# Moving elementwise work between VectorE, GpSimd and ScalarE in a fused attention, convolution and MLP kernel

## The chip, the cores and the metric

One core of a Trainium2 chip runs the whole program. The metric is the device time of one execution in microseconds; the median of several executions is compared.

## The reference

Three blocks follow one another. The batch is 4, the sequence 544 (32 global and 512 local tokens), the width 512.

1. Attention: 8 heads of 64; global queries see all keys, local queries see the global keys and a window of 32 to each side.
2. A gated MLP with a convolution: `h = relu(x @ w_in)` to 1024 columns, a convolution of three taps over the sequence, `sigmoid` of it as a gate, `(h * gate) @ w_out` back to 512.
3. A block with a Fourier transform over sequence and features, of which the real part is added: `u = x + real(fft(fft(x)))`, then a layer norm, `relu(un @ w_ch1) @ w_ch2` through 2048 columns (the dense MLP), and `u + ch`.

The weights and most other inputs reach the kernel as float64 in HBM and are turned into float32 on the chip.

## The kernel before, in words

**Precision.** Products are made in float32 halves: a value is split into a high part in float32r (a rounded copy by ScalarE) and the rest (value minus high part, a subtraction of two tensors), and `mm3` (L144) makes three matmuls of the two. So each weight tile and each activation needs a copy and a two-tensor subtraction.

**Weights.** `fetch` (L177) loads 128 x 512 float64 values as pairs of int32; `from_f64` (L161) makes float32 of them in place. Its steps: ScalarE takes the absolute value of the head word (L163); a clamp to the range of float32 (L164); the tail word is shifted right by 29 bits (L168 on VectorE, or L166 on ScalarE as an arithmetic scaling); VectorE joins both (L170); VectorE puts the sign in (L175), or ScalarE makes a sign tensor (L172) and GpSimd multiplies by it (L173). `put` (L201) then makes the high part by ScalarE (L203) and the rest by GpSimd (L204). There are 16 such tiles for `w_in` and `w_out` (`make_w`, L427; for `w_out` a sum and a difference of halves come between, L433 and L434) and 32 for `w_ch1` and `w_ch2` (`make_c`, L698, one tile, and `make_cs`, L713, two or three tiles at once with L719 in place of L204). The intermediate value lies in `mag`, of which there are two buffers; late in the kernel three buffers cut from `misc` take their place.

**Stages.** The first loop (L543) runs over 32 halves of head pairs plus two. Each step makes scores (`s_mm`), a masked maximum on VectorE (L279), the exponential on ScalarE (L291), a scaling on GpSimd (L302), transposes on TensorE, copies out of PSUM (L321) and the product with the values. In steps 0 to 7 the tiles of `w_in` and `w_out` are converted beside it. From step 10 on each step also does two units of the gated MLP (64 units in all): `m_g1` (first product, L453 evacuates on ScalarE), `m_conv` (three taps: L464 or L466 for the middle one, L467, L468), `m_tanh` (L474), `m_gate` (L485 to L487) and `m_g2` (second product). From unit 52 the middle tap is on ScalarE (L464), before on VectorE (L466).

A second loop (L820) ends the gated MLP; the first batch's transform (`fft`, L616) and the first layer norm (`ln(0)`, L724) run beside it, and the first eight tiles of `w_ch1` are fetched and converted. The third loop (L859) is the dense MLP: 128 units in 8 pieces of half a batch (`c_g1` L767, evacuated by L779 and L780; `c_g2` L783, accumulated over 16 units and finished by L800, L801). In its first five units the transforms of the other three batches and the next twelve conversions are done, in the next units the last twelve; `ln(c + 1)` runs in the midst of piece `c`.

**The transform.** `fft` folds a batch into its even and odd parts (L623, L626 on GpSimd, L627 one row on VectorE), splits these (L624, L625, L628, L629), multiplies with cosine and sine tables over features and then tokens, evacuates (L642 to L650, L663 to L676) and adds and subtracts the results into `u` (L677 on VectorE, L678 on GpSimd). `ln` sums features (L733, L734), multiplies by ones on TensorE, subtracts the mean (L742), splits (L743, L744 on GpSimd), squares (L747) and sums again (L749, L750), and makes the reciprocal root (L760, L761). `ln(1)` and later use the space of the last transform's input as scratch.

**What sets the order.** In the first loop the order of TensorE and of the DMA queue of SyncE is that of the program text; on the other engines, and on all engines after that loop, a planner places instructions by the priorities of the table at L21 and by its own estimates of time. Each engine then executes its list in order. All large loads are issued on SyncE's queue, the transform's tables on GpSimd's (L805).

Of the kernel before, what the change touches and what calls it, by code (L numbers as in the profile page):

```python
# [28 lines left out]
NF = 274  # L29
# [95 lines left out]
def fused_kernel(ctx: ExitStack, tc: tile.TileContext, d, out):  # L125
# [35 lines left out]
    def from_f64(raw, mag, clamp=None, tail_act=False, sign_act=False):  # L161
        head, tail = raw[:, :, 1], raw[:, :, 0]
        act.activation(mag, f32(head), AF.Abs, scale=65536.0)  # L163
        (clamp or dve).tensor_scalar(mag, mag, 2.0, TOP, op0=ALU.max, op1=ALU.min)  # L164
        if tail_act:
            act.activation(tail, tail.bitcast(U32), AF.Copy, scale=0.999 * 2.0**-29, bias=-0.499)  # L166
        else:
            dve.tensor_scalar(tail, tail, 29, None, op0=ALU.logical_shift_right)  # L168
        val = bits(mag)
        dve.scalar_tensor_tensor(val, val, 3, tail, op0=ALU.logical_shift_left, op1=ALU.bitwise_or)  # L170
        if sign_act:
            act.activation(f32(head), f32(head), AF.Sign)  # L172
            gp.tensor_mul(mag, mag, f32(head))  # L173
        else:
            dve.scalar_tensor_tensor(val, head, -(2**31), val, op0=ALU.bitwise_and, op1=ALU.bitwise_or)  # L175
# [25 lines left out]
    def put(pool, tag, val):  # L201
        t = pool.tile([128, 2, 512], F32R, tag=tag, name="w_" + tag)
        act.copy(t[:, 0], val)  # L203
        gp.tensor_sub(t[:, 1], val, f32(t[:, 0]))  # L204
        return t
# [220 lines left out]
    @prio("w")  # L426
    def make_w(i):  # L427
        val = unpack(mp, w_raw.pop(i), gp if i >= 8 else dve)
        if i < 8:
            w_in[i] = put(wp, f"w{i}", val)  # L430
            return
        eo = mp.tile([128, 512], F32, tag="mag", name="mag", bufs=2)
        dve.tensor_add(eo[:, 0:256], val[:, 0:256], val[:, 256:512])  # L433
        gp.tensor_sub(eo[:, 256:512], val[:, 0:256], val[:, 256:512])  # L434
        w_out[i - 8] = put(wp, f"w{i}", eo)
# [20 lines left out]
    def m_conv(u):  # L456
# [6 lines left out]
        if u >= 52:  # L463
            act.mul(y, hb[:, cc:cc + HS], convw2[:, m, 1:2])  # L464
        else:
            dve.tensor_scalar(y, hb[:, cc:cc + HS], convw2[:, m, 1:2], None, op0=ALU.mult)  # L466
# [149 lines left out]
    def fft(b):  # L616
# [6 lines left out]
        gp.tensor_add(fe, eo[:, 0:2, 0:NF], eo[:, 0:2, rev])  # L623
        act.copy(fh[:, 0:2], fe)  # L624
        gp.tensor_sub(fl[:, 0:2], fe, f32(fh[:, 0:2]))  # L625
        gp.tensor_sub(fd, eo[:, 2:4, 0:NF], eo[:, 2:4, rev])  # L626
        dve.tensor_add(fd[0:1, 0], eo[0:1, 2, 0:NF], eo[0:1, 2, rev])  # L627
        act.copy(fh[:, 2:4], fd)  # L628
        gp.tensor_sub(fl[:, 2:4], fd, f32(fh[:, 2:4]))  # L629
# [26 lines left out]
        for c in range(2):  # L656
# [21 lines left out]
            gp.tensor_sub(ut[:, 2 + c, 0:S], e[:, 0:S], q[:, 0:S])  # L678
# [18 lines left out]
    @prio("cv")  # L697
    def make_c(i):  # L698
        t = put(*c_slot(i), unpack(mp, w_raw.pop(i), dve, i > 15, i % 3 == 0))
        if i < 16:  # L700
            ch1[i] = t
        else:
            ch2[i - 16] = t
# [8 lines left out]
    @prio("cv")  # L712
    def make_cs(i, k):  # L713
        raw = w_raw.pop(i)
        vals = [unpack(mp, raw[:, j], dve, True, (i + j) % 3 == 0) for j in range(k)]
        t = fp.tile([128, k, 2, 512], F32R, tag=f"v{i}", name="ws")
        for j in range(k):
            act.copy(t[:, j, 0], vals[j])
            gp.tensor_sub(t[:, j, 1], vals[j], f32(t[:, j, 0]))  # L719
            ch2[i + j - 16] = t[:, j]  # L720
# [3 lines left out]
    def ln(c):  # L724
# [8 lines left out]
        gp.tensor_add(s4, ut[:, 0:2], ut[:, 2:4])  # L733
        gp.tensor_add(s4[:, 0], s4[:, 0], s4[:, 1])  # L734
# [9 lines left out]
        gp.tensor_sub(cl, cf, f32(ch))  # L744
# [4 lines left out]
        gp.tensor_add(s4, cf[:, 0:2], cf[:, 2:4])  # L749
        gp.tensor_add(s4[:, 0], s4[:, 0], s4[:, 1])  # L750
# [175 lines left out]
```

## Time and profile before

| what | value |
|---|---|
| median of 3 runs | 882.42 us (882.37 to 883.85) |
| the profiled execution | 884.08 us, of which 881.9 us span |
| TensorE busy (matmul) | 803.3 us, mean granted clock 0.940 |
| VectorE busy | 505.4 us, 1222 instructions |
| ScalarE busy | 347.4 us, 884 instructions |
| GpSimd busy | 308.6 us, 318 instructions |

The span goes from the first to the last instruction of the profiled execution; what lies around it belongs to the execution's time too. In the rows PE is TensorE's matmuls, PEld its weight loads, DVE VectorE, ACT ScalarE, POOL GpSimd, SP SyncE. L164 is line 164 of the kernel before. The granted clock is TensorE's, as a share of 2.4 GHz. A group's idle time is that of its engine just before these instructions, with what ended most of it.

### The profile page before, as it was taken

The page shows a single profiled execution, that of the slowest core. Times are in us where ns is not written, and L with a number is a line of the kernel's source. Part 1 is how long each engine was busy: PE and PEld are TensorE (multiplying, and loading weights), DVE is VectorE, ACT ScalarE, POOL GpSimd, SP SyncE. Part 2 cuts the span into 40 slices and gives each one's busy share as a digit, 9 for nine tenths or more (in the row PEclk, how much of TensorE's full clock was granted, in tenths as well). Part 3 has the DMA queues.
Part 4 walks back from the last instruction along what each step waited for, and adds up shares of the span by engine and source line. Part 5 has one row for each costly group of instructions (what it writes and reads, how often), then busy time and mean ns, then how long its engine had stood idle before and what let it go on. Part 6 is the DMA issues. An engine that isn't in the chain of part 4 may idle for free. (4 is left out here: it accounts for less than half of the span.)

```text
span 881.9 us, 16202 instructions
## 1 busy us (share of the span) xinstructions
PE 803.3 (91%) x6436; PEld 752.0 (85%) x6436; DVE 505.4 (57%) x1222; ACT 347.4 (39%) x884; POOL 308.6 (35%) x318
## 2 busy tenths in 40 slices
PE   5767999999999999987779489999999999999997
PEld 3445788999899899877678388999999999999997
DVE  5786977686778767899788973221222222222212
ACT  4555555555555534555446552112121212121110
POOL 4878622132222222564676656022130404030100
PEclk8776999999999999989779699999999999999999
DMA  9460111101010012253304300000000000000000
GB/s 315 139 205 15 72 34 53 60 29 58 30 59 29 2 40 66 72 165 99 143 0 159 129 1 26 1 26 1 14 14 1 26 1 27 1 26 1 27 1 25
DMA packets 25387, 48.33 MB, mean 55 GB/s; under 512 B 1960, under 2 KB 18728, under 8 KB 25312
## 3 DMA queue, kind: packets, MB, share of 16 engines
q1 hardware_dynamic: 24480, 44.66, 15.0%
q0 software_dynamic: 832, 2.65, 1.2%
q8 instruction: 50, 0.82, 0.4%
q14 instruction: 25, 0.20, 0.1%
HBM read 43.23 MB, written 4.46 MB: 54 GB/s over the span
## 5 line engine op out<-in xcount | busy, mean ns | idle before, releaser
L302 POOL TENSOR_SCALAR pb<-pb,sm 128x224 f32<-128x224 f32 x128 | 72.9, 585 | 153.0 <-DVE sm L297 107.0
L142 PE MATMUL ps_a<-hdt,w_v 128*128 128x272 f32 x864 | 122.1, 290 | 0.0
L142 PE MATMUL ps_a<-g,w_w 128*128 128x272 f32 x768 | 114.1, 295 | 6.2 <-ACT g L486 4.4
L142 PE MATMUL ps_g<-xh,w_w 128*128 128x274 f32 x512 | 115.0, 303 | 0.0
L142 PEld LDWEIGHTS ps_a<-hdt,w_v 128*128 128x128 f32 x864 | 114.6, 191 | 0.0
L142 PE MATMUL ps_pv<-chl,w_w 128*128 128x272 f32 x768 | 109.7, 291 | 4.0 <-DVE hdt L780 3.8
L142 PE MATMUL ps_g<-chl,w_w 128*128 128x272 f32 x768 | 109.1, 290 | 2.4 <-DVE hdt L780 2.4
L142 PEld LDWEIGHTS ps_a<-g,w_w 128*128 128x128 f32 x768 | 103.2, 192 | 8.0 <-ACT g L486 5.2
L142 PEld LDWEIGHTS ps_pv<-chl,w_w 128*128 128x128 f32 x768 | 102.1, 191 | 5.3 <-issue 4.1
L142 PEld LDWEIGHTS ps_g<-chl,w_w 128*128 128x128 f32 x768 | 101.8, 190 | 3.1 <-DVE hdt L780 3.1
L780 DVE SCALAR_TENSOR_TENSOR hdt<-ps_pv,hdt 128x272 fp32r<-128x272 f32 x64 | 28.2, 440 | 122.0 <-ACT hdt L779 121.9
L142 PE MATMUL ps_a<-hdt,ws 128*128 128x272 f32 x672 | 92.5, 287 | 1.7 <-POOL ws L719 1.7
L801 POOL TENSOR_TENSOR misc<-misc,u 128x272 f32<-128x272 f32 x28 | 19.3, 720 | 212.6 <-DVE misc L800 212.6
L142 PEld LDWEIGHTS ps_g<-xh,w_w 128*128 128x128 f32 x512 | 86.7, 193 | 7.7 <-issue 4.4
L780 DVE SCALAR_TENSOR_TENSOR hdt<-ps_g,hdt 128x272 fp32r<-128x272 f32 x64 | 28.0, 437 | 109.2 <-ACT hdt L779 109.2
L142 PEld LDWEIGHTS ps_a<-hdt,ws 128*128 128x128 f32 x672 | 87.2, 188 | 1.9 <-POOL ws L719 1.9
L779 ACT ACTIVATE hdt<-ps_g 128x272 fp32r<-128x272 f32 x64 | 25.4, 397 | 128.1 <-PE ps_g L142 125.5
L779 ACT ACTIVATE hdt<-ps_pv 128x272 fp32r<-128x272 f32 x64 | 25.3, 395 | 128.0 <-PE ps_pv L142 127.1
L142 PE MATMUL ps_g<-xl,w_w 128*128 128x274 f32 x256 | 75.2, 294 | 0.0
L291 ACT ACTIVATE pb<-pb,sm 128x224 f32<-128x224 f32 x128 | 60.2, 472 | 15.6 <-DVE sm L279 15.6
L474 ACT ACTIVATE y<-y 128x272 f32<-128x272 f32 x64 | 27.5, 430 | 76.2 <-DVE y L468 76.2
L142 PE MATMUL ps_s<-qk 64*128 64x224 f32 (+1 forms) x144 | 40.1, 431 | 16.4 <-DVE smg L373 9.3
(211 smaller groups left out, 1489.4 us busy)
## 6 DMA issues: line engine op xcount, KB each, us to landing
qk<-in_qk_dram SPq DMA_DIRECT2D x16, 592.0 KB, 5.6
raw_w<-in_ch_dram SPq DMA_DIRECT2D x16, 512.0 KB, 3.8
v<-in_v_dram SPq DMA_DIRECT2D x8, 640.0 KB, 4.8
raw_v<-in_ch_dram SPq DMA_DIRECT2D x9, 512.0 KB, 5.8
out_dram<-misc SPq DMA_DIRECT2D x32, 136.0 KB, 1.8
raw_w<-in_w_in_dram SPq DMA_DIRECT2D x8, 512.0 KB, 5.1
raw_w<-in_w_out_dram SPq DMA_DIRECT2D x8, 512.0 KB, 4.0
raws<-in_ch_dram SPq DMA_DIRECT2D x7, 512.0 KB, 5.1
```

Source lines behind the costliest of these rows:

```text
L142: return pe.matmul(o, a, b, start=start, stop=stop)
L291: act.activation(p, p, AF.Exp, bias=sm[:, k:k + 1], scale=-1.0, accum_out=sm[:, 4 + k:5 + k])
L302: gp.tensor_scalar(p, p, sm[:, k:k + 1], 1.0, op0=ALU.mult, op1=ALU.mult)
L474: act.activation(g_t[u], g_t[u], AF.Tanh, scale=0.5)
L779: act.activation(hd[:, 0], o, AF.Relu)
L780: dve.scalar_tensor_tensor(hd[:, 1], o, 0.0, f32(hd[:, 0]), op0=ALU.max, op1=ALU.subtract)
L801: (dve if c == 7 else gp).tensor_add(o, o, u_t[b][:, e, HS * half:HS * half + HS])
```

## The change

Two-tensor additions and subtractions go from GpSimd to VectorE in the weight conversions, the transforms, and the layer norm of piece 0 (`eng` in `ln`; later pieces stay on GpSimd). The clamps of all 48 weight tiles are done by GpSimd (16 of them in `make_w`, of which 8 were there before). The shift of the tail word goes to ScalarE for all 32 tiles of `w_ch1` and `w_ch2` (before: the 16 of `w_ch2`) and for the even ones of the 16 of `w_in` and `w_out` (before: none). The variant with a sign tensor, used by every third tile of the 32, is gone: VectorE puts all signs in. All middle taps of the convolution are on ScalarE. The clamp's two operations are written in the other order.

```diff
-    def from_f64(raw, mag, clamp=None, tail_act=False, sign_act=False):
+    def from_f64(raw, mag, clamp=None, tail_act=False):
...
-        (clamp or dve).tensor_scalar(mag, mag, 2.0, TOP, op0=ALU.max, op1=ALU.min)
+        (clamp or dve).tensor_scalar(mag, mag, TOP, 2.0, op0=ALU.min, op1=ALU.max)
...
-        if sign_act:
-            act.activation(f32(head), f32(head), AF.Sign)
-            gp.tensor_mul(mag, mag, f32(head))
-        else:
-            dve.scalar_tensor_tensor(val, head, -(2**31), val, op0=ALU.bitwise_and, op1=ALU.bitwise_or)
+        dve.scalar_tensor_tensor(val, head, -(2**31), val, op0=ALU.bitwise_and, op1=ALU.bitwise_or)
...
     def put(pool, tag, val):
-        gp.tensor_sub(t[:, 1], val, f32(t[:, 0]))
+        dve.tensor_sub(t[:, 1], val, f32(t[:, 0]))
...
     def make_w(i):
-        val = unpack(mp, w_raw.pop(i), gp if i >= 8 else dve)
+        val = unpack(mp, w_raw.pop(i), gp, i % 2 == 0)
...
-        gp.tensor_sub(eo[:, 256:512], val[:, 0:256], val[:, 256:512])
+        dve.tensor_sub(eo[:, 256:512], val[:, 0:256], val[:, 256:512])
...
     def m_conv(u):
-        if u >= 52:
-            act.mul(y, hb[:, cc:cc + HS], convw2[:, m, 1:2])
-        else:
-            dve.tensor_scalar(y, hb[:, cc:cc + HS], convw2[:, m, 1:2], None, op0=ALU.mult)
+        act.mul(y, hb[:, cc:cc + HS], convw2[:, m, 1:2])
...
     def fft(b):
-        gp.tensor_add(fe, eo[:, 0:2, 0:NF], eo[:, 0:2, rev])
+        dve.tensor_add(fe, eo[:, 0:2, 0:NF], eo[:, 0:2, rev])
         act.copy(fh[:, 0:2], fe)
-        gp.tensor_sub(fl[:, 0:2], fe, f32(fh[:, 0:2]))
-        gp.tensor_sub(fd, eo[:, 2:4, 0:NF], eo[:, 2:4, rev])
+        dve.tensor_sub(fl[:, 0:2], fe, f32(fh[:, 0:2]))
+        dve.tensor_sub(fd, eo[:, 2:4, 0:NF], eo[:, 2:4, rev])
...
-        gp.tensor_sub(fl[:, 2:4], fd, f32(fh[:, 2:4]))
+        dve.tensor_sub(fl[:, 2:4], fd, f32(fh[:, 2:4]))
...
-            gp.tensor_sub(ut[:, 2 + c, 0:S], e[:, 0:S], q[:, 0:S])
+            dve.tensor_sub(ut[:, 2 + c, 0:S], e[:, 0:S], q[:, 0:S])
...
     def make_c(i):
-        t = put(*c_slot(i), unpack(mp, w_raw.pop(i), dve, i > 15, i % 3 == 0))
+        t = put(*c_slot(i), unpack(mp, w_raw.pop(i), gp, True))
...
     def make_cs(i, k):
-        vals = [unpack(mp, raw[:, j], dve, True, (i + j) % 3 == 0) for j in range(k)]
+        vals = [unpack(mp, raw[:, j], gp, True) for j in range(k)]
...
-            gp.tensor_sub(t[:, j, 1], vals[j], f32(t[:, j, 0]))
+            dve.tensor_sub(t[:, j, 1], vals[j], f32(t[:, j, 0]))
...
     def ln(c):
+        eng = gp if c else dve
-        gp.tensor_add(s4, ut[:, 0:2], ut[:, 2:4])
-        gp.tensor_add(s4[:, 0], s4[:, 0], s4[:, 1])
+        eng.tensor_add(s4, ut[:, 0:2], ut[:, 2:4])
+        eng.tensor_add(s4[:, 0], s4[:, 0], s4[:, 1])
...
-        gp.tensor_sub(cl, cf, f32(ch))
+        eng.tensor_sub(cl, cf, f32(ch))
...
-        gp.tensor_add(s4, cf[:, 0:2], cf[:, 2:4])
-        gp.tensor_add(s4[:, 0], s4[:, 0], s4[:, 1])
+        eng.tensor_add(s4, cf[:, 0:2], cf[:, 2:4])
+        eng.tensor_add(s4[:, 0], s4[:, 0], s4[:, 1])
```

## Rows read from the trace of the kernel before

**Rows 1.** Stretches: busy us (count) of PE, PEld, DVE, ACT, POOL, then granted clock

```profile
22.00:110.00 88.00, 66.42 (x508) 50.98 (x504) 69.51 (x199) 48.23 (x133) 67.16 (x71) 0.77 0.33 108
132.00:330.00 198.00, 198.00 (x1855) 181.60 (x1855) 147.59 (x465) 106.72 (x324) 46.67 (x85) 1.00 0.12 39
330.00:540.00 210.00, 170.60 (x1150) 156.69 (x1150) 177.22 (x278) 108.92 (x221) 122.92 (x80) 0.88 0.27 89
375.00:419.00 44.00, 35.71 (x228) 32.55 (x227) 43.92 (x69) 25.71 (x53) 24.16 (x14) 0.88 0.43 132
485.00:507.00 22.00, 8.98 (x47) 7.55 (x47) 21.55 (x23) 12.16 (x22) 15.24 (x10) 0.61 0.35 130
540.00:870.00 330.00, 330.00 (x2640) 330.00 (x2640) 77.69 (x159) 60.48 (x137) 55.15 (x55) 1.00 0.04 13
```

**Rows 2.** What TensorE waited for, 330 to 540: total us, times, longest

```profile
PE ps_t L142 <- DVE hdt L736: 9.7, 2, 8.9
```

**Rows 3.** Order of time, 483.5 to 487: start us, us, instruction

```profile
483.94 1.85 POOL L678 TENSOR_TENSOR u<-u 128x544 f32<-128x544 f32 x1
484.50 1.57 DVE L164 TENSOR_SCALAR misc<-misc 128x512 f32<-128x512 f32 x1
```

**Rows 4.** Durations of L164 and L677, whole span: min/median/max ns

```profile
L164 DVE TENSOR_SCALAR misc<-misc x24: 406/414/2732, 404.0 to 528.6; 128x512 f32<-128x512 f32 x24
L164 POOL TENSOR_SCALAR mag<-mag x8: 1913/1915/2462, 15.1 to 101.1; 128x512 f32<-128x512 f32 x8
L677 DVE TENSOR_TENSOR u<-u x8: 706/1205/1903, 361.2 to 490.4; 128x544 f32<-128x544 f32 x8
```

**Rows 5.** Order of time at two GpSimd clamps, 27.5 to 30.6, 100.9 to 103

```profile
27.89 2.46 POOL L164 TENSOR_SCALAR mag<-mag 128x512 f32<-128x512 f32 x1 [0.80 <-ACT mag L163]
27.90 0.68 DVE L175 SCALAR_TENSOR_TENSOR mag<-raw_w,mag 128x512 int32<-128x512 int32 x1
...
101.05 1.92 POOL L164 TENSOR_SCALAR mag<-mag 128x512 f32<-128x512 f32 x1 [0.80 <-ACT mag L163]
101.09 0.87 DVE L467 SCALAR_TENSOR_TENSOR y<-h,convw,y 128x272 f32<-128x272 f32 x1
```

**Rows 6.** Groups of VectorE, 330 to 540: busy us, mean ns, idle before

```profile
L164 DVE TENSOR_SCALAR misc<-misc 128x512 f32<-128x512 f32 x24 | 18.5, 772 | 5.8 <-ACT misc L163 5.8
L164 DVE TENSOR_SCALAR mag<-mag 128x512 f32<-128x512 f32 x8 | 6.5, 810 | 0.0
L168 DVE TENSOR_SCALAR raw_w<-raw_w 128x512 int32<-128x512 int32 x16 | 10.7, 673 | 1.8 <-DMA raw_w<-in_ch_dram 1.8
L170 DVE SCALAR_TENSOR_TENSOR mag<-mag,raw_w 128x512 int32<-128x512 int32 x8 | 5.4, 680 | 0.0
L677 DVE TENSOR_TENSOR u<-u 128x544 f32<-128x544 f32 x8 | 10.2, 1277 | 0.0
```

**Rows 7.** Tile y, two stretches: busy us (count) of DVE, ACT, then granted clock

```profile
132.00:330.00 198.00, 95.39 (x201) 33.89 (x80) 1.00 0.12 39
330.00:540.00 210.00, 44.12 (x66) 19.43 (x44) 0.88 0.27 89
```

**Rows 8.** Busy time of L170, then of L175, 330 to 540

```profile
330.00:540.00 210.00, 29.73 (x32) 0.88 0.27 89
330.00:540.00 210.00, 21.80 (x21) 0.88 0.27 89
```

**Rows 9.** Groups of GpSimd, 330 to 540

```profile
L744 POOL TENSOR_TENSOR chl<-u,chl 128x1088 fp32r<-128x1088 f32 x3 | 10.4, 3452 | 7.0 <-ACT chl L743 7.0
```

**Rows 10.** Groups of GpSimd, 0 to 132

```profile
L204 POOL TENSOR_TENSOR w_w<-mag,w_w 128x512 fp32r<-128x512 f32 x16 | 22.2, 1395 | 5.6 <-ACT w_w L203 2.8 <-issue 2.7
L164 POOL TENSOR_SCALAR mag<-mag 128x512 f32<-128x512 f32 x8 | 16.4, 2054 | 5.4 <-ACT mag L163 5.3
L434 POOL TENSOR_TENSOR mag<-mag 128x256 f32<-128x256 f32 x8 | 6.6, 826 | 6.3 <-DVE sm L296 3.8 <-DVE sm L297 1.6 <-DVE mag L175 0.7
```

**Rows 11.** What VectorE waited for, 0 to 132: total us, times, longest

```profile
DVE mag L170 <- POOL mag L164: 3.0, 1, 3.0
```

## The prediction, made before the changed kernel was seen

> **What bounds the kernel now.** I read the table of stretches first [rows 1]. From 132 to 330 us and from 540 to 870 us TensorE is busy without a break at granted clock 1.00, which is its upper level, 2.4 GHz: nothing that is done on VectorE, ScalarE or GpSimd can shorten these 528 us. What can move is the start (22 to 110: TensorE 66.4 of 88, clock 0.77) and the middle (330 to 540: 170.6 of 210, clock 0.88). In the middle VectorE is busy 177.2 of 210 us, and 43.9 of 44 and 21.6 of 22 in the two densest pieces; in the second of these TensorE works 9 of 22 us at 0.61, mostly its lower level of 1.2 GHz, after standing idle. Then I read who TensorE waits for there: the longest wait, 8.9 us, is for VectorE's L736 [rows 2]. So the middle is paced by VectorE, and the reader should ask what VectorE's time consists of.
>
> A part of it is waiting inside its instructions. In order of time [rows 3]: GpSimd's subtraction L678 runs from 483.94 to 485.79; VectorE's clamp L164 starts at 484.50 and is done at 486.07, 0.28 us after GpSimd. It took 1.57 us where its median is 0.41 [rows 4]. So beside a two-tensor instruction of GpSimd VectorE's instruction stood until that ended. The change takes most of these away. Whether it puts something as bad in their place is seen where GpSimd clamps already [rows 5]: its clamp ran from 27.89 to 30.35, and VectorE's two-tensor L175, started 0.01 us after it, took 0.68 us, as long as such an instruction takes undisturbed (0.680, the row of L170 on mag in [rows 6]). At 101.05 a second clamp ran 1.92 us; L467, started 0.04 us after, took 0.87 us, longer than the 0.475 that its kind takes on average from 132 to 330 [rows 7], but not the 1.9 of the clamp. The clamp itself can lose: 2.46 us against a median of 1.92 [rows 4].
>
> Against this speaks a rule of the Trainium skill, page "SBUF — State Buffer", section "SBUF: two separate sides": GpSimd's instruction and a VectorE instruction with two SBUF inputs take one port pair as an exclusive lock for their whole length. By it the longer clamps would block as the additions do. The two clamps above disagree; it is rival A.
>
> **The change part by part, on VectorE in the middle stretch.**
> 1. Clamps to GpSimd: 32 leave, 18.5 + 6.5 = 25.0 us [rows 6]. Shifts to ScalarE: 16 leave, 10.7 us [rows 6]. Together 35.7 us.
> 2. Waiting that ends inside what stays. L170: 29.73 us for 32, at 0.680 each 21.8, so 8.0 waiting; L175: 21.80 for 21, so 7.5 [rows 8]. L677: 8 × (1.277 − 0.706) = 4.6 [rows 4, 6]. The convolution and gate (tile y): 0.668 us each here (44.12 over 66) against 0.475 (95.39 over 201) in 132 to 330, where GpSimd did almost no two-tensor work [rows 7]; 66 × 0.19 is 12.8, of which I take 10, since the short middle tap is a fifth of the instructions there and rare here. Sum 30. What stays on GpSimd are the layer norms of pieces 1 and up, whose L744 is 10.4 us for three [rows 9], and the final additions, about a tenth of its 122.9 us [rows 1]. So 27 us of waiting go.
> 3. Added: 32 subtractions of 512 columns at 0.68 = 21.8; the sign by VectorE for the 11 tiles that used ScalarE and GpSimd, 11 × 0.68 = 7.5; the FFTs' six additions of 544 to 548 columns for four batches, 24 × 0.71 (the undisturbed L677 [rows 4]) = 17.0; the layer norm of piece 0, 0.71 + 0.44 + 1.4 + 0.71 + 0.44, scaled by columns, about 3.6. Together 49.9.
> Net: 49.9 − 35.7 − 27 = −12.8 us of VectorE's time. The bounds: none of the waiting goes, +14; all of it goes and the moved additions cost only 0.6, about −20. I take the middle, as the two clamps and the L678 row lie on that side. VectorE is busy in 84% of the stretch, so the stretch gives back 0.84 × 12.8 = **10.8 us**. TensorE allows it: it idles 39.4 us there, and some more is lost to the clock.
>
> GpSimd loses about 100 of its 122.9 us and gets 32 clamps at about 2.05 (mean of eight [rows 10]), 65.6 us: it stays below half busy. ScalarE gets 16 shifts and is rid of 11 signs on the same shape, at 108.9 of 210 [rows 1]: nothing, as long as VectorE is the fuller engine.
>
> The new waits: a tile's second VectorE step now waits for a GpSimd clamp and its last for a ScalarE copy. Behind a waiting VectorE stand the convolution, the FFT evacuations and L780, so TensorE. Eight clamps on GpSimd cost VectorE one wait of 3.0 us [rows 11], 0.38 each: 32 would cost 12. Today VectorE waits for ScalarE before its own clamp; that goes to GpSimd. From −6 to +12, I take zero: seven of eight cost nothing. In the three-buffer part a tile's chain grows by 1.9 − 0.4 for the clamp and shrinks by 1.4 − 0.7 for the subtraction; that 0.8 us I cost at nothing, since loads and conversions stand several tiles ahead, and with that cover gone 12 us at most (16 tiles).
>
> **The start (0 to 132).** GpSimd loses 16 subtractions (22.2) and 8 halves (6.6) and gets 8 clamps (16.4): −12.4 us [rows 10]. VectorE gets 16 × 0.68 and 8 halves at some 0.4, 14.1, and loses 8 clamps and 8 shifts (6.6 at 0.41 each), the taps and some waiting: about even. Neither is full (67 and 70 of 88 [rows 1]); TensorE's order is written by hand there and follows the chain maximum, exponential, scaling, transpose. From −10 (GpSimd paces it) to +4 (new clamps ahead of the scalings in its queue), I take **−2**, nearer zero, as both engines have idle time.
>
> **Middle taps and 132 to 330.** 40 taps go to ScalarE, 106.7 of 198 busy; at 0.42, its mean on tile y (33.89 over 80 [rows 7]), that is 17 us more. TensorE, busy throughout, covers it; without that cover it would be those 17 us at most. Transfers are not moved between queues.
>
> Sum: −10.8 − 2 = −12.8. The profiled execution took 884.08 us, 881.9 of them the span; 884.1 − 12.8 = 871.3. The median of the runs, 882.42, lies 1.7 below it, so **869.6**.
>
> **Rivals.**
> A. The clamps hold VectorE up as the additions did. Waiting was 30 plus 16 in the removed instructions (35.7 − 48 × 0.41), 46 us per 122.9 of GpSimd work, 0.37; 65.6 us of clamps bring 24.5 back. VectorE then has 11.7 more, times 0.84 is +10: about **892**, slower. It decides from the point where VectorE's two-tensor instructions that start under a clamp end behind it. For: the page's rule and L467's 0.87. Against: L175's 0.68.
> B. VectorE stands behind clamps and copies in its queue, 12 us as above: the gain is gone, **882** (880 to 887). For: the one wait of 3.0. Against: seven without.
> C. GpSimd paces the start and all 12.4 us come out there: a further 10, **859**. For: 67 of 88 busy. Against: VectorE is as busy.
> D. VectorE isn't what ends the middle, but its chain of dependences; then the gain is that of shorter chains only, two or three us: 879. I count it with B.
>
> **Numbers.** Forecast 0.52 (860 to 879), A 0.10, B with D 0.22, C 0.16. Range 853 to 887: it takes in C and B and leaves out A and the deepest of C. This measurement can tell 0.2%, 1.8 us. Faster: 0.52 + 0.16 + a quarter of B is 0.73; within: a quarter of B, 0.06; slower: A and half of B, 0.21.
>
> **What would show it.** Right: in the middle L170 and L175 average about 0.7, VectorE's busy time falls by about 13, GpSimd's to near 80, and dense work at clock 1.00 without break begins near 529 instead of 540. Wrong: L170 and L467 of 1.5 us beside L164 on GpSimd (A); idle VectorE before L170 with L164 as the releaser (B); all of the gain before 132 (C); VectorE relieved and the middle as long as before (D). A TensorE order in the middle that is not today's, since the order there is planned, would shift all of it by some us either way.

## The result and the profile after

The changed kernel takes 850.08 us (median of four runs, 849.81 to 850.16) against 882.39 us: ratio 0.9636 [0.9614, 0.9657]. The direction was forecast, the size was not: −32 us where −12.8 was written, and below the range's lower end of 853. The profiled executions have spans of 881.9 and 847.9 us; the first of them took 884.08 us, 1.7 above its kernel's median, so the spans differ by 34.0 us and the medians by 32.3.

In the changed kernel the join is L170, the sign L171, the high copy L199, the subtraction of a weight split L200 (L712 in `make_cs`), the transforms' folds L616 to L622, the sums into `u` L670 and L671, the layer norm's lines 6 lower than before. First the stretches, by the page's head and by windows of the changed kernel; the columns are those of [rows 1], with the DMA engines' share and their GB/s behind the clock.

```profile
PE 788.3 (93%) x6436; PEld 739.9 (87%) x6436; DVE 474.9 (56%) x1202; ACT 380.9 (45%) x949; POOL 197.4 (23%) x262
```

```profile
20.70:98.00 77.30, 58.48 (x469) 44.14 (x470) 65.28 (x200) 52.33 (x142) 36.68 (x55) 0.82 0.37 125
120.20:317.80 197.60, 197.60 (x1851) 181.18 (x1851) 137.38 (x430) 128.07 (x365) 44.93 (x83) 1.00 0.12 40
317.80:506.50 188.70, 163.36 (x1159) 151.91 (x1158) 162.88 (x297) 113.51 (x230) 49.22 (x44) 0.93 0.30 98
506.50:836.00 329.50, 329.50 (x2636) 329.50 (x2635) 77.09 (x157) 59.83 (x135) 52.52 (x52) 1.00 0.04 13
```

The unbroken stretches are as long as before (198 and 330 us), and the second begins at 506.5 us, where the forecast said near 529; all of the gain lies in the start and the middle, where the forecast looked for it. To compare kernels at the same points of the work and not at the same times, I cut **the start** from 20 us to ScalarE's evacuation of the gated MLP's unit 8, and **the middle** from that of unit 48 to the 25th evacuation of the dense MLP. Of the kernel before, and then of the changed one:

```profile
20.00:130.60 110.60, 87.35 (x685) 69.95 (x684) 87.48 (x251) 60.92 (x172) 75.43 (x83) 0.79 0.28 93
327.60:559.90 232.30, 192.90 (x1329) 178.99 (x1328) 183.31 (x290) 112.34 (x230) 132.10 (x92) 0.89 0.26 85
```

```profile
20.00:118.80 98.80, 79.16 (x673) 62.79 (x674) 83.71 (x256) 67.05 (x184) 43.72 (x65) 0.86 0.31 104
315.40:525.80 210.40, 185.06 (x1332) 173.61 (x1332) 168.81 (x309) 116.98 (x239) 55.07 (x53) 0.94 0.29 94
```

The start is 11.8 us shorter (forecast 2), the middle 21.9 (forecast 10.8); together with 0.3 us in between that is the whole 34.0 of the spans. VectorE's busy time in the middle fell by 14.5 us, close to the 12.8 of the forecast. TensorE's idle time (length less busy time) fell from 39.4 to 25.3 us there, and its busy time by 7.8 us for the same matmuls (1329 and 1332 records), at a granted clock of 0.94 for 0.89.

What answers to [rows 2], TensorE's waits in the changed kernel's middle:

```profile
PE ps_a L142 <- DVE w_v L200: 8.9, 3, 8.0
PE ps_a L142 <- DVE ws L712: 4.7, 2, 3.2
```

The 8.9 us for the layer norm of piece 0 are gone; the longest wait, 8.0 us, is now for a converted weight tile. To [rows 4] and [rows 10] answer the clamps, in durations over the whole span (min/median/max ns) and as a group up to 120 us:

```profile
L164 POOL TENSOR_SCALAR mag<-mag x24: 611/614/1535, 12.8 to 394.2; 128x512 f32<-128x512 f32 x24
L164 POOL TENSOR_SCALAR misc<-misc x24: 611/932/3679, 385.8 to 491.1; 128x512 f32<-128x512 f32 x24
```

```profile
L164 POOL TENSOR_SCALAR mag<-mag 128x512 f32<-128x512 f32 x16 | 10.9, 686 | 14.7 <-ACT mag L163 14.2
```

A GpSimd clamp took 1.92 us before; undisturbed it now takes 0.61, with its two operations in the other order. And to [rows 3] and [rows 5] answers a stretch in which clamps and two-tensor instructions of VectorE stand side by side (start us, us, instruction):

```profile
420.86 4.26 POOL L164 TENSOR_SCALAR misc<-misc 128x512 f32<-128x512 f32 x2 [1.36 <-ACT misc L163]
420.90 0.71 DVE L618 TENSOR_TENSOR fl<-ff,fh 128x548 fp32r<-128x548 f32 x1
421.54 0.68 DVE L170 SCALAR_TENSOR_TENSOR misc<-misc,raw_w 128x512 int32<-128x512 int32 x1
422.14 0.68 DVE L200 TENSOR_TENSOR w_w<-misc,w_w 128x512 fp32r<-128x512 f32 x1
422.74 0.72 DVE L619 TENSOR_TENSOR ff<-u 128x548 f32<-128x548 f32 x1
423.38 0.68 DVE L171 SCALAR_TENSOR_TENSOR misc<-raw_w,misc 128x512 int32<-128x512 int32 x1
424.57 1.08 DVE L170 SCALAR_TENSOR_TENSOR misc<-misc,raw_w 128x512 int32<-128x512 int32 x1 [0.51 <-POOL misc L164]
```

Two clamps that need 1.2 us alone took 4.26, while VectorE's five instructions, one behind the other without a break, ran at their usual 0.68 to 0.72; only the last, which came in under the second clamp, was held, for 0.4 us. The loser here is GpSimd, and nobody waits long for it.

### The profile page after: what moved, and what is told of

It reads as the page before. It is cut to its first block, busy times and chain, and to the rows that moved or that the text cites. A ratio compares the mean times of both kernels' runs of the same rounds, so it can differ in the third digit from the quotient of the medians.

```text
span 847.9 us, 16080 instructions
## 1 busy us (share of the span) xinstructions
PE 788.3 (93%) x6436; PEld 739.9 (87%) x6436; DVE 474.9 (56%) x1202; ACT 380.9 (45%) x949; POOL 197.4 (23%) x262
## 4 chain that ended last, share of the span: by engine, by line
PE 76%; DVE 12%; DMA 6%; ACT 2%; issue 2%; POOL 0%; SPq 0%; DVEq 0%; ACTq 0%; POOLq 0%
PE ps_a L142 32%; PE ps_g L142 20%; PE ps_pv L142 13%; PE ps_s L142 6%; PE ps_t L142 2%; DMA raw_w<-in_w_in_dram 2%; DVE misc L171 1%; DVE mag L170 1%; DMA raw_w<-in_w_out_dram 1%; DVE w_w L200 1%; DMA co<-in_co_dram 1%; DMA raw_w<-in_ch_dram 1%; DVE mag L171 1%; DVE pb L275 1%; DVE misc L170 1%
## 5 line engine op out<-in xcount | busy, mean ns | idle before, releaser
L142 PE MATMUL ps_a<-hdt,w_v 128*128 128x272 f32 x864 | 125.0, 294 | 8.9 <-DVE w_v L200 8.9
L142 PEld LDWEIGHTS ps_a<-hdt,w_v 128*128 128x128 f32 x864 | 116.8, 194 | 9.7 <-DVE w_v L200 9.7
L142 PE MATMUL ps_a<-g,w_w 128*128 128x272 f32 x768 | 110.9, 291 | 0.5 <-DVE g L480 0.5
L142 PE MATMUL ps_g<-chl,w_w 128*128 128x272 f32 x768 | 108.1, 288 | 2.1 <-DVE hdt L774 2.1
L142 PE MATMUL ps_pv<-chl,w_w 128*128 128x272 f32 x768 | 106.8, 288 | 0.1
L142 PEld LDWEIGHTS ps_a<-g,w_w 128*128 128x128 f32 x768 | 100.7, 188 | 1.5 <-DVE g L480 0.8
L142 PEld LDWEIGHTS ps_pv<-chl,w_w 128*128 128x128 f32 x768 | 100.3, 188 | 0.3 <-DVE hdt L774 0.3
L773 ACT ACTIVATE hdt<-ps_g 128x272 fp32r<-128x272 f32 x64 | 25.4, 397 | 132.0 <-PE ps_g L142 125.1
L773 ACT ACTIVATE hdt<-ps_pv 128x272 fp32r<-128x272 f32 x64 | 25.3, 396 | 132.2 <-PE ps_pv L142 128.2
L142 PEld LDWEIGHTS ps_g<-xl,w_w 128*128 128x128 f32 x256 | 48.9, 191 | 0.0
```

What stands on the lines that cost most here:

```text
L142: return pe.matmul(o, a, b, start=start, stop=stop)
L773: act.activation(hd[:, 0], o, AF.Relu)
```

## The experiments

Two theories stood at the outset. The **order theory**: the cheap clamp explains the surplus, as the forecast had priced it at 2.05 us. The **relief theory**: what VectorE and GpSimd no longer do to one another, in long single instructions on the way to TensorE, is worth more than the forecast's VectorE time. All kernels with their lengths and, for the middle, the busy times of VectorE and GpSimd (us, from windows cut as above). Differences in the text are of medians unless a ratio is named; the kernel before, measured beside each group of runs, had medians of 880.7 to 882.7.

| kernel | median | ratio to before | start | middle | VectorE | GpSimd |
|---|---|---|---|---|---|---|
| before | 882.4 | 1 | 110.6 | 232.3 | 183.3 | 132.1 |
| after | 850.1 | 0.9636 [0.9614, 0.9657] | 98.8 | 210.4 | 168.8 | 55.1 |
| after, old clamp order | 858.4 | 0.9737 [0.9715, 0.9760] | 102.9 | 215.0 | 170.3 | 94.3 |
| before, new clamp order | 880.3 | 0.9973 [0.9956, 0.9990] | 108.1 | 232.2 | 183.4 | 132.0 |
| change at the first 16 tiles alone | 865.4 | 0.9838 [0.9793, 0.9883] | 98.3 | 224.8 | 183.5 | 135.2 |
| change at all but those | 858.2 | 0.9736 [0.9710, 0.9761] | 106.4 | 211.6 | 167.3 | 54.9 |
| after, taps back on VectorE | 852.7 | 0.9673 [0.9649, 0.9697] | 97.8 | 213.6 | 169.8 | 54.1 |
| after, clamps all on VectorE | 861.7 | 0.9782 [0.9754, 0.9811] | 103.7 | 217.3 | 170.8 | 26.0 |
| after, transforms back on GpSimd | 857.5 | 0.9728 [0.9705, 0.9751] | 99.9 | 216.6 | 170.4 | 95.4 |
| before, additions moved alone | 863.5 | 0.9786 [0.9756, 0.9816] | 105.8 | 218.8 | 177.9 | 43.4 |
| after, additions back on GpSimd | 874.1 | 0.9924 [0.9901, 0.9947] | 104.1 | 231.3 | 169.3 | 136.8 |
| before, another order (fev) | 879.0 | 0.9973 [0.9957, 0.9988] | 110.3 | 227.7 | 186.1 | 134.0 |
| before, another order (f3) | 878.5 | 0.9984 [0.9965, 1.0002] | 109.3 | 228.7 | 187.3 | 135.9 |
| after, another order (fev) | 852.7 | 0.9684 [0.9666, 0.9702] | 98.9 | 213.3 | 166.9 | 53.3 |
| before, scores doubled | 886.6 | 1.0057 [1.0035, 1.0080] | 117.8 | 227.0 | 184.2 | 134.3 |
| after, layer norm of piece 1 moved too | 847.9 | 0.9615 [0.9591, 0.9638] | 100.9 | 207.8 | 166.7 | 45.0 |

**The clamp's order, undone in the changed kernel and done alone in the kernel before.**

```diff
-        (clamp or dve).tensor_scalar(mag, mag, TOP, 2.0, op0=ALU.min, op1=ALU.max)
+        (clamp or dve).tensor_scalar(mag, mag, 2.0, TOP, op0=ALU.max, op1=ALU.min)
```

> The changed kernel with the clamp's two operations in the order of before (max with 2.0 first, then min with TOP); all else as changed. In the changed kernel's trace a GpSimd clamp of 128x512 takes 0.61 us where none disturbs it, against 1.91 us before. Theory order: the part of the gain that was not forecast (some 19 of 32 us) comes from this; a clamp takes 1.9 us again, the first relu of the gated MLP comes 4 to 8 us later than in the changed kernel, and the kernel takes 862 to 872 us. Rival relief: what counts is that two-tensor work left GpSimd, which has room for slow clamps; the clamp takes 1.9 us, but the kernel 850 to 855 us.

> The kernel before with only the order of the clamp's two operations changed (min with TOP first). Only 8 of its 48 weight clamps are on GpSimd, all in the first 110 us. Theory order: these 8 take 0.6 to 0.7 us instead of 2.05, GpSimd loses 11 us of 67 between 22 and 110 us, and the kernel gains 3 to 10 us (872 to 879). Rival relief: the start isn't paced by GpSimd's time but by VectorE waiting beside its additions: 880 to 883.

With the old order the changed kernel takes 858.44 us, between the two theories: the cheap form is worth 8.4 us, about a quarter of the gain, and 24 remain without it. The durations of that kernel's clamps:

```profile
L164 POOL TENSOR_SCALAR mag<-mag x24: 1913/2012/2817, 13.3 to 398.5; 128x512 f32<-128x512 f32 x24
L164 POOL TENSOR_SCALAR misc<-misc x24: 1909/2062/4686, 390.0 to 500.4; 128x512 f32<-128x512 f32 x24
```

In the kernel before the same swap gives 2.4 us by its ratio, as only eight clamps are on GpSimd and all lie in the start (108.1 for 110.6). The price of 2.05 in the forecast was right for the form that stood in the rows, and wrong for the form in the diff.

**What in the form is slow.** Instructions behind the end of the changed kernel, three times each, and in a second kernel two of each of other forms:

```diff
+    gp.tensor_scalar(dst, scr, 2.0, TOP, op0=ALU.max, op1=ALU.min)
+    gp.tensor_scalar(dst, scr, TOP, 2.0, op0=ALU.min, op1=ALU.max)
+    gp.tensor_scalar(dst, scr, 2.0, 4.0, op0=ALU.max, op1=ALU.min)
+    gp.tensor_scalar(dst, scr, 4.0, 2.0, op0=ALU.min, op1=ALU.max)
+    gp.tensor_scalar(dst, scr, 2.0, 1.0, op0=ALU.mult, op1=ALU.mult)
+    gp.tensor_tensor(dst, scr, dst, op=ALU.add)
```

> The changed kernel with 18 GpSimd instructions of 128x512 appended behind its end, three each of: max with 2.0 then min with TOP; min with TOP then max with 2.0; max with 2.0 then min with 4.0; min with 4.0 then max with 2.0; multiplication twice; addition of two tensors. Theory order: the first operation decides; max first takes 1.9 us with either bound, min first 0.6, the multiplications 0.6 to 0.8, the addition 1.3. Rival value: the large bound TOP matters; max first with 4.0 takes 0.6 too. The kernel's time grows by the appended work and says nothing else.

> The changed kernel with sixteen more GpSimd instructions behind its end (two each of six two-operation forms on 128x512 and of the two clamps on 128x256); only their durations count. In the changed kernel max with 2.0 and then min takes 1.92 us, min and then max 0.61. If a maximum as the first operation is what is slow, max then mult and max then max take 1.9 and min last takes 0.6 behind a mult. If a minimum as the second operation is slow, mult then min and min then min take 1.9, and max then mult 0.6. If only the pair max, min in this order is slow, all six take 0.6. At half the width 1.0 against 0.3 if the cost is per column.

Order of time on GpSimd in the first (three instructions a line, in the order of the diff, with 0.08 us between two, so that 5.92 is 3 × 1.92 and 2.01 is 3 × 0.61):

```profile
848.13 5.92 POOL L880 TENSOR_SCALAR misc<-misc 128x512 f32<-128x512 f32 x3 [47.42 <-DMA out_dram<-misc]
854.13 2.01 POOL L882 TENSOR_SCALAR misc<-misc 128x512 f32<-128x512 f32 x3
856.22 5.91 POOL L884 TENSOR_SCALAR misc<-misc 128x512 f32<-128x512 f32 x3
862.21 2.01 POOL L886 TENSOR_SCALAR misc<-misc 128x512 f32<-128x512 f32 x3
864.30 2.02 POOL L888 TENSOR_SCALAR misc<-misc 128x512 f32<-128x512 f32 x3
866.41 3.94 POOL L890 TENSOR_TENSOR misc<-misc 128x512 f32<-128x512 f32 x3
```

And in the second (two a line; the first of six forms that took the same, then the two clamps at half the width):

```profile
847.36 3.93 POOL L879 TENSOR_SCALAR misc<-misc 128x512 f32<-128x512 f32 x2 [47.43 <-DMA out_dram<-misc]
...
871.42 2.21 POOL L891 TENSOR_SCALAR misc<-misc 128x256 f32<-128x256 f32 x2
873.71 0.88 POOL L893 TENSOR_SCALAR misc<-misc 128x256 f32<-128x256 f32 x2
```

The value plays no part (4.0 for the largest float32 changes nothing), the order does. All three explanations of the second run fell: maximum and multiplication, multiplication and minimum, minimum and multiplication, multiplication and maximum, two maxima, two minima all take 1.92 us. Of the forms tried only minimum then maximum and multiplication twice take 0.61. Which other pairs are fast wasn't tried.

**The start alone, and everything else alone.**

```diff
-    def put(pool, tag, val):
+    def put(pool, tag, val, eng=gp):
...
-            w_in[i] = put(wp, f"w{i}", val)
+            w_in[i] = put(wp, f"w{i}", val, dve)
```

> The kernel before with the change made only for the 16 tiles of the first block (w_in, w_out): clamps on GpSimd in the new order, every second shift on ScalarE, subtractions and the difference of halves on VectorE. Transforms, layer norm, taps and the 32 later tiles as before. By the milestones of the two traces (first relu of the gated MLP 8.3 us earlier, unit 8 11.8 us earlier, unchanged until unit 48) the start brings 10 to 13 us: 869 to 873. If the taps on ScalarE brought part of it (units 0 to 8 came 3.5 us closer together), 873 to 877.

> The changed kernel with the 16 tiles of the first block converted as before (8 clamps on VectorE, 8 on GpSimd, all shifts on VectorE, subtractions on GpSimd; the clamp keeps the new order). Transforms, layer norm, taps and the 32 later tiles as changed. If start and middle are separate stages whose gains add, it loses what the start brought with its subtractions: 856 to 862. If the start's gain came from the clamp's order alone, which this kernel keeps, it stays at 850 to 854.

The first is the kernel before with the first 16 tiles converted as in the changed one, the second the reverse. The start's 12.3 us come with the first alone, and the second keeps 20.7 of the middle's 21.9. So each stretch owns its gain. But the first missed its expectation (its four runs lie between 863.8 and 872.1, and the window is from the fastest): its middle, whose work it doesn't touch, is 7.5 us shorter too, in another order of the planner. That raised the question of the orders, below.

**Orders.** One number of the priority table is changed (in the third kernel `'f3'` from 200 to 0 instead); every instruction and its engine stay.

```diff
-PRIORITY = {'s': 50, 'ex': 50, 't': 50, 'ev': 50, 'glo': 400, 'w': 50, 'me': 100, 'mg1': 200, 'cv': 200, 'fft': 100, 'f3': 200, 'fev': 200, 'cev': 400}
+PRIORITY = {'s': 50, 'ex': 50, 't': 50, 'ev': 50, 'glo': 400, 'w': 50, 'me': 100, 'mg1': 200, 'cv': 200, 'fft': 100, 'f3': 200, 'fev': 12, 'cev': 400}
```

> The kernel before with one number of the planner's priority table changed ('fev', the transforms' evacuations, 200 to 12): every instruction is there as before, but from the end of the first loop on TensorE, VectorE and ScalarE get other orders. Disputed: how much of the gain of 22 us in the middle is a lucky new order. If orders are worth many us, this kernel is off by more than 6 us, faster as well as slower being possible. If the instructions and their engines decide, it stays within 4 us of before (878 to 886).

> The changed kernel with the same number of the priority table changed. If the changed kernel's order is a lucky one, another order loses 6 us or more (over 856). If not, within 4 us of it (846 to 854), and the distance to the kernel before in the same order stays some 32 us.

> The kernel before with another number of the table changed ('f3', the later transforms' steps, 200 to 0). As for the first re-ordering: within 4 us of before if the instructions and their engines decide, off by more than 6 us if orders are worth many us.

All three stay near their originals: the kernel before gains 2.4 and 1.4 us by its ratios, the changed one loses 2.6 (4.2 by the ratios). In the middle the three orders of the kernel before take 227.7 to 232.3 us, the two of the changed one 210.4 and 213.3. Averaged over the orders the middle's gain is 229.6 − 211.9 = 17.7 us, so about 4 of its 21.9 us may be the order's. Two more kernels of the table have the instructions of before in their middle, in other orders: the one with the first 16 tiles changed (224.8) and the one with the scores doubled (227.0). With them the orders of before spread over 7.5 us, and between the shortest of these middles and the longer one of the changed kernel, 213.3, 11.5 us remain: so far as these orders show, that much at least is not the order's. The start varies less: where its instructions and their order are the same, profiled executions took 109.3 to 110.6 us of the kernel before and 98.8 to 100.9 of the changed one.

**Taps, clamps and transforms put back, one at a time, in the changed kernel.**

```diff
-        act.mul(y, hb[:, cc:cc + HS], convw2[:, m, 1:2])
+        if u >= 52:
+            act.mul(y, hb[:, cc:cc + HS], convw2[:, m, 1:2])
+        else:
+            dve.tensor_scalar(y, hb[:, cc:cc + HS], convw2[:, m, 1:2], None, op0=ALU.mult)
```

> The changed kernel with the middle taps of units 0 to 51 back on VectorE. Theory: 44 of the 52 units run while TensorE is busy without break, and the start of the run that changed only the conversions, with taps on VectorE, was as long as in the changed kernel (98.3 against 98.8 us from 20 us to unit 8), so the taps bring nothing: 849 to 852. Rival: ScalarE's taps take VectorE's load off the first units: 853 to 856.

```diff
-        (clamp or dve).tensor_scalar(mag, mag, TOP, 2.0, op0=ALU.min, op1=ALU.max)
+        dve.tensor_scalar(mag, mag, TOP, 2.0, op0=ALU.min, op1=ALU.max)
```

> The changed kernel with all clamps on VectorE. Theory (VectorE's time counts): 48 clamps of 0.41 us come to it, 13 us in the middle and 6.6 in the start; at the rates of the forecast that costs 11 and 3 us: 860 to 866. Rival (the clamp's move pays for nothing, two-tensor work leaving GpSimd is all): the chain of a tile gets shorter by one change of engine and GpSimd holds nothing against VectorE any more: 847 to 853.

```diff
-        dve.tensor_add(fe, eo[:, 0:2, 0:NF], eo[:, 0:2, rev])
+        gp.tensor_add(fe, eo[:, 0:2, 0:NF], eo[:, 0:2, rev])
...
-            dve.tensor_sub(ut[:, 2 + c, 0:S], e[:, 0:S], q[:, 0:S])
+            gp.tensor_sub(ut[:, 2 + c, 0:S], e[:, 0:S], q[:, 0:S])
```

> The changed kernel with the transforms' folds, splits and last subtraction back on GpSimd (24 two-tensor instructions of 544 to 548 columns). VectorE is rid of 17 us. Theory relief (a two-tensor instruction on GpSimd stops VectorE's for its whole length): the waiting comes back, and the kernel is slower by 4 to 12 us: 854 to 862. Rival (GpSimd has room, 49 of 189 us in the middle, and VectorE is the fuller engine): 844 to 849, faster than the changed kernel.

The taps are worth 2.6 us, no more than another order is, so the forecast's zero isn't contradicted. The clamps on GpSimd are worth 11.6 us, 4.9 in the start and 6.9 in the middle; yet with the clamps back on VectorE its busy time in the middle is only 2.0 us longer (170.8 for 168.8). The transforms' six additions for four batches are worth 7.4 us, and VectorE's busy time differs by 1.5. Both landed where they were expected, but the table says that the reason wasn't VectorE's sum of time. In the middle each is worth 6 to 7 us, though, which is also what orders differ by. The next pair tests the reason.

**The additions alone, and everything but the additions.** In the kernel before only the subtractions and additions go to VectorE (`put`, `make_w`, `fft`, `make_cs`, `ln(0)`); in the other kernel just these are put back on GpSimd in the changed one.

```diff
-        gp.tensor_sub(t[:, 1], val, f32(t[:, 0]))
+        dve.tensor_sub(t[:, 1], val, f32(t[:, 0]))
...
-        gp.tensor_add(s4, ut[:, 0:2], ut[:, 2:4])
+        eng = gp if c else dve
+        eng.tensor_add(s4, ut[:, 0:2], ut[:, 2:4])
```

> The kernel before with only the two-tensor additions and subtractions moved to VectorE (weight splits, halves, transforms, layer norm of piece 0); clamps, shifts, signs and middle taps stay where they were. By VectorE's time alone: some 41 us of waiting inside its instructions go and some 42 us of instructions come, so 878 to 884 us. If what stalls TensorE is single long instructions of VectorE and GpSimd in the chain (the relief theory), it gains without the clamps too: 862 to 874.

> The changed kernel with all two-tensor additions and subtractions back on GpSimd (weight splits, halves, transforms, layer norm of piece 0); clamps in the new order on GpSimd, shifts and taps on ScalarE, signs on VectorE. The additions alone gave 18.5 of the 32 us. If the parts add up, this one gives the other 13.5: about 868 to 870. If the two-tensor instructions on GpSimd are what holds everything up and the clamps there only help once those are gone, 874 to 882. If VectorE's time alone counted, clamps and shifts of 36 us less 7 us of signs would bring 20 us or more: under 863.

The additions alone give 18.9 us (by the ratio), as the relief theory had it; everything else alone gives 6.7, as the theory of dependence had it, and a third of what VectorE's time would have. Together they give 32.1, so 6.5 us seem to be there only when both are done; orders differ by as much, so this isn't settled. The middle of the first and of the second kernel, columns as in [rows 1]:

```profile
322.40:541.20 218.80, 190.32 (x1332) 177.66 (x1332) 177.94 (x350) 112.54 (x229) 43.41 (x32) 0.91 0.28 91
```

```profile
320.50:551.80 231.30, 191.98 (x1332) 178.75 (x1332) 169.32 (x252) 117.13 (x242) 136.78 (x113) 0.90 0.27 86
```

This is the sharpest result of the study. In the second kernel VectorE's busy time fell by 14.0 us, as much as in the changed one, and the middle is 1.0 us shorter. In the first VectorE's fell by 5.4 and the middle by 13.5. VectorE's busy time doesn't set the middle's length. (Each is one order: 231.3 lies among the middles of the kernel before, 224.8 to 232.3, and 218.8 lies 6.0 below the shortest of them.) The waits of TensorE in the second kernel show what does:

```profile
PE ps_t L142 <- DVE hdt L730: 10.5, 1, 10.5
PE ps_a L142 <- POOL ws L712: 8.1, 3, 4.9
```

The longest ends at 479.7 us. It is the wait of [rows 2] again, for the first step of the layer norm of piece 0. GpSimd's order of time before it, then VectorE's last step:

```profile
468.65 1.05 POOL L164 TENSOR_SCALAR misc<-misc 128x512 f32<-128x512 f32 x1
469.96 1.41 POOL L200 TENSOR_TENSOR w_w<-misc,w_w 128x512 fp32r<-128x512 f32 x1 [0.26 <-ACT w_w L199]
471.33 1.79 POOL L727 TENSOR_TENSOR u<-u 128x544 f32<-128x544 f32 x1
473.08 1.73 POOL L200 TENSOR_TENSOR w_v<-misc,w_v 128x512 fp32r<-128x512 f32 x1
474.77 1.05 POOL L164 TENSOR_SCALAR misc<-misc 128x512 f32<-128x512 f32 x1
475.80 0.76 POOL L728 TENSOR_TENSOR u<-u 128x272 f32<-128x272 f32 x1
...
478.70 0.84 DVE L730 TENSOR_TENSOR hdt<-u,hdt 128x272 fp32r<-128x272 f32 x1
```

TensorE stood still while the layer norm's sums (L727, L728) queued on GpSimd among weight conversions, and its last step behind VectorE's conversions: of the 10.5 us the first 7.4, to 476.56, passed with L727 and L728 on GpSimd's list. In the kernel before it was similar, in other lines: a subtraction of a weight tile, the layer norm's two sums and more subtractions on GpSimd; then, on VectorE, L684, which writes the last of what L733 reads, and the line that [rows 2] names:

```profile
491.30 1.57 POOL L204 TENSOR_TENSOR w_v<-misc,w_v 128x512 fp32r<-128x512 f32 x1 [1.33 <-ACT w_v L203]
492.84 1.51 POOL L733 TENSOR_TENSOR u<-u 128x544 f32<-128x544 f32 x1
494.43 1.09 POOL L734 TENSOR_TENSOR u<-u 128x272 f32<-128x272 f32 x1
...
497.51 3.16 POOL L204 TENSOR_TENSOR w_v<-misc,w_v 128x512 fp32r<-128x512 f32 x2
```

```profile
491.68 0.42 DVE L684 TENSOR_TENSOR u<-u,ps_t 1x273 f32<-1x273 f32 x1
...
498.03 1.50 DVE L736 TENSOR_TENSOR hdt<-u,hdt 128x272 fp32r<-128x272 f32 x1
```

The releaser that the view of waits names is the last step of the chain, L736 on VectorE. But of the 8.9 us, which end at 499.7 us, the 3.4 from L684's end at 492.10 to 495.52 lay on GpSimd's list, and L736 itself took 1.50 us beside GpSimd's subtractions, for 0.84 in the other kernel and 0.38 in the median of its eight. The pair shows that the additions on GpSimd hold the middle up. How much of that is their own time in the chain, and how much the stretching of VectorE's steps beside them, it doesn't separate, as both went together.

**TensorE's clock.** The kernel before with more work for TensorE in the start:

```diff
-                mm(sb[h][:, a], t[r, q0:q0 + 128], t[r, k0:k0 + 224], True, True)
+                for _ in range(2 if i < SOLO else 1):
+                    mm(sb[h][:, a], t[r, q0:q0 + 128], t[r, k0:k0 + 224], True, True)
```

> The kernel before with the score matmuls of the first eight steps done twice (64 matmuls more, the same result), everything else as it was. Disputed: whether the granted clock of the start (0.77 to 0.82 in the two kernels) is a cost of its own that depends on how much TensorE has to do there, or only goes along with its waiting. Clock theory: with more work between the waits the granted clock of the stretch rises above 0.85, the matmuls that are not doubled get shorter by several us in sum, and the kernel is within -5 to +2 us of before (877 to 884) although it does more. Rival: the clock stays near 0.77, the doubled matmuls cost their time, and the kernel is 5 to 15 us slower (887 to 897).

Neither came out. Its start, columns as in [rows 1]:

```profile
20.00:137.80 117.80, 90.63 (x761) 73.23 (x758) 93.89 (x264) 63.08 (x183) 72.83 (x86) 0.87 0.31 103
```

The granted clock rose from 0.79 to 0.87 and TensorE's busy time by only 3.3 us for the added matmuls; but the start became 7.2 us longer, 3.9 of it idle. The kernel is 5 us slower (its middle came out 5.3 us shorter, about what another order is worth). So a higher granted clock alone doesn't shorten this start. The kernel before in its first other order (fev) says the same: its start has the instructions and the order of before, and at a clock of 0.83 and with 85.5 us of TensorE's time it is as long (110.3 us). How much of the 16 us by which TensorE's busy time shrank in the changed kernel (8.2 and 7.8) is a gain of its own stays open.

**A version that goes one step further.** In the changed kernel the two-tensor instructions that are left on GpSimd, those of the layer norms of pieces 1 and up, still hold VectorE:

```profile
457.50 1.33 POOL L727 TENSOR_TENSOR u<-u 128x544 f32<-128x544 f32 x1
457.56 1.82 DVE L170 SCALAR_TENSOR_TENSOR misc<-misc,raw_v 128x512 int32<-128x512 int32 x1 [0.51 <-POOL misc L164]
...
469.58 2.73 POOL L738 TENSOR_TENSOR chl<-u,chl 128x1088 fp32r<-128x1088 f32 x1 [3.50 <-ACT chl L737]
...
469.83 3.03 DVE L171 SCALAR_TENSOR_TENSOR misc<-raw_v,misc 128x512 int32<-128x512 int32 x1
```

```diff
-        eng = gp if c else dve
+        eng = gp if c > 1 else dve
```

> The changed kernel with the two-tensor additions and the subtraction of ln(1) also on VectorE (ln(2) and later stay on GpSimd). In the changed kernel ln(1)'s L727 and L738 on GpSimd are the last that hold VectorE up in the middle (L170 of 1.82 us at 457.6, L171 of 3.03 us at 469.8 where 0.68 is usual): some 3.5 us of waiting go, and some 4.5 us of instructions come. If the waiting matters because it stands in the chain to TensorE, 845 to 849 us; if VectorE's time is all that counts, 849 to 852; beyond that either way a new order of the planner is at work.

It takes 847.91 us. The middle is 2.6 us shorter, from 210.4 to 207.8, and the joins and signs of that stretch take 0.67 to 0.98 us. The start, which it doesn't touch, came out 2.1 us longer (100.9). The total is 2 us below the changed kernel's, but the intervals of the two ratios overlap and another order is worth as much: the fastest kernel of the study, by a margin that isn't settled.

## Why the prediction was wrong

**Right: what VectorE gains.** The steps 1 to 3 of the middle gave −12.8 us; measured −14.5 (183.31 to 168.81). That it came out so near is partly luck, as two misses in step 2 cancel. L170's waiting went as written, for the most part: its group in the middle is 24.05 us for 32, or 0.75 each, where it was 0.93 [rows 8]. The sign's did not: L171 is still 0.92 each (29.52 for 32), which at 0.68 undisturbed leaves 7.8 us of waiting where L175 had 7.5, 2.35 of them in the row at 469.83 alone, under a subtraction that stayed on GpSimd. In its place the convolution and the gate gave more than the 10 us taken: VectorE's time on tile y fell from 46.04 us (68 instructions) to 29.05 (64) from the one middle to the other.

```profile
317.80:506.50 188.70, 24.05 (x32) 0.93 0.30 98
...
317.80:506.50 188.70, 29.52 (x32) 0.93 0.30 98
```

**Wrong: "So the middle is paced by VectorE", and from it "the stretch gives back 0.84 × 12.8 = 10.8 us".** This is the step that failed. The pair of kernels above separates the two: 14.0 us less of VectorE with the additions left on GpSimd shorten the middle by 1.0, and 5.4 less with the additions gone shorten it by 13.5. In its place the runs show chains that go through several engines, with GpSimd's list of subtractions of 1.3 to 1.8 us in them (GpSimd busy 132.1 of 232.3 us); what is taken from one engine comes out only as far as the other isn't next in the chain. The forecast counted what GpSimd's instructions cost VectorE, and gave GpSimd's own 100 us that went nothing, since it was "below half busy" afterwards. It read [rows 2] as a wait for VectorE; the wait ended there, but 3.4 of its 8.9 us passed on GpSimd's list, and L736 took 1.50 us instead of 0.38 beside GpSimd's subtractions.

**Wrong: the start, "I take −2, nearer zero, as both engines have idle time".** Measured −11.8; the bound −10, which was also rival C, was nearer. But C's reason (GpSimd paces the start) isn't the whole: the additions alone took 25.7 us from GpSimd there and gave 4.8, everything else alone took 9.4 from it and 5.1 from VectorE and gave 6.5. With 67 and 70 of 88 us busy, idle time of two engines in a chain need be no slack, as each can wait while the other works. This reading is argued; no run takes the start's chain apart, and its cause stays open.

**Wrong: the clamp "at about 2.05".** It takes 0.61 us undisturbed in the form of the diff. The diff showed the new order, and the text had the row for the old one. This is 8.4 us of the result; with it undone, the kernel is at 858.4, within the range but still 11 us under the forecast. GpSimd, which the forecast left near 80 us busy in its stretch, is at 49.2 from 317.8 to 506.5.

**Not in the sum: TensorE's busy time.** It fell by 16 us (granted clock 0.79 to 0.86 and 0.89 to 0.94) for the same matmuls, but for 12 that run before 20 us in the changed kernel and so outside its start. The text says that some more is lost to the clock, and gives it no term.

**The smaller steps.** The new waits were taken as zero: VectorE's for a clamp are 1.0 us in two waits in the changed kernel's middle (L170 on GpSimd's L164), so zero was right. Middle taps at zero: 2.6 us by the run, within what an order does.

**The rivals.** A, clamps that hold VectorE as the additions did, fell: of the rows from 420.86 on, one in six two-tensor instructions was held, for 0.4 us. A clamp does hold VectorE, but only near the clamp's own start. The kernel with the old order, whose clamps are three times as long, shows it:

```profile
420.98 1.91 POOL L164 TENSOR_SCALAR misc<-misc 128x512 f32<-128x512 f32 x1
421.04 1.09 DVE L170 SCALAR_TENSOR_TENSOR misc<-misc,raw_v 128x512 int32<-128x512 int32 x1 [0.33 <-POOL misc L164]
422.05 0.68 DVE L200 TENSOR_TENSOR w_v<-misc,w_v 128x512 fp32r<-128x512 f32 x1
```

L170 was held for 0.41 us, as beside a clamp of 0.61, and L200 behind it ran at its usual 0.68 within the same clamp. Beside a two-tensor instruction of GpSimd VectorE stood to the end: L171 at 469.83 took 3.03 us, until L738 was done and 0.55 beyond. By the Trainium skill, "SBUF — State Buffer", section "SBUF: two separate sides", such a pair locks out the other for the whole instruction. The trace agrees with that where GpSimd's instruction has two tensors, and not where it has one, the clamp.

B and D fell with the 1.0 us of waits and the shorter middle; D's idea, a chain of dependences ends the middle, was nearer the truth than the forecast, but I took it that shorter instructions on VectorE alone shorten the chain. The gain of faster GpSimd steps on that chain had no rival at all.

## What to carry to other kernels

When TensorE's longest wait ends on a busy engine, follow the chain back to the other engines before pricing the change by that engine's busy time: here 14 us less of VectorE were worth 1 us while GpSimd's subtractions stayed in the chain, and 13.5 us of the middle came with a VectorE that was hardly emptier. Take the price of an instruction from a row of its exact form, the order of its two operations included, and if there is no such row, let the range say so. Where a planner orders the work, run the same instructions in another order or two first: here that is worth up to 7.5 us of the middle, and smaller differences there prove nothing.

## What the runs showed of the hardware that was not expected

On GpSimd a two-operation instruction with scalars on 128 x 512 float32 takes 0.61 us as minimum then maximum or as two multiplications, and 1.92 us in the seven other pairs tried, maximum then minimum among them; at half the width 0.40 and 1.06. An addition of two tensors of that size takes 1.26 us there, undisturbed.

A clamp of GpSimd holds VectorE's two-tensor instruction by 0.4 us, whether the clamp takes 0.61 us (at 424.50) or 1.91 (at 420.98 in the kernel with the old order). While VectorE's two-tensor instructions follow one another without a break it is the clamp that gives way: 4.26 us for two that take 1.2 alone. Under a two-tensor instruction of GpSimd VectorE stands until the end, 3.03 us beside a 2.73 us L738.
